# An explicit order for 1944 steps of a two-filter S4 mix, paired sines over two PSUM banks, and no sine product on GpSimd

## The chip, the cores and the metric

The kernel runs on one core of one Trainium2 chip. The metric is the device time of one execution in microseconds (us); the median of several runs is compared. The profile and the trace show one further execution.

## The reference, cut to what matters

Two state-space filters, A (S4) and B (S4D), act on the same signal x of 2048 positions and 512 channels; a sigmoid gate per position mixes the results.

```python
P = jnp.exp(logdA[:, :, None] * l[None, None, :])      # 512 channels x 128 modes x 2048 positions
K = jnp.einsum("dn,dnl,dn->dl", Cc, P, dB).real        # the filter of A; B alike, with 2 * C
Uf = rfft(up); Kf = rfft(Kp)                           # both padded to 2 * L
y = irfft(Uf * Kf)[:, :L] + u * Dskip
g = _sigmoid((x * gate_w).sum(-1, keepdims=True))
return g * a + (1 - g) * b
```

The bulk of the work is to build the filter K, 512 x 2048 sums over 128 complex modes, and the long convolution of x with it. All of it is float32.

## The kernel before, in words

**Tiling.** The 512 channels are cut into four quarters q of 128 channels. Each quarter has two filters k (0 is A, 1 is B), so there are eight units (q, k). A unit's 128 channels are worked in eight chunks of 16 channels. The 128 modes lie on the partitions. A position is split as 64 j + s, so that the exponential at a position is a product of two tables, one over 32 values of j (an angle times j, and a decay) and one over 64 values of s. The sum over the modes then is a matmul of two tables.

**A chunk** (`chunk`, from line 519) runs over all engines. GpSimd writes the two angle tables into a buffer `x` (lines 553 and 562, int32, 512 columns each) and the decay tables into a buffer `E` (lines 573 and 581, 512 and 1024 columns). ScalarE takes four sines of 512 columns: `sf` and `sc` of the angles (lines 591 and 592), then the absolute value in place (line 593, 1024 columns), then `cf` and `cc`, the cosines by a shifted sine (lines 595 and 599). Three of the four go to PSUM buffers `ps`. VectorE multiplies them by the decays: two products of `sf` into `Qt` (lines 603 and 606), one of `sc` into `Dt` (line 612), a double one of `cf` into `Pt` (line 616, 1024 columns) and one of `cc` into `Ct` (line 621). In 28 of the 64 chunks, chosen by the bit masks `DP`, `sc` goes to an SBUF buffer `scs` and GpSimd makes `Dt` from it. TensorE then forms the filter's values (`products`, line 638, 32 small matmuls) and adds the skip term with one matmul by the identity (line 647). ScalarE copies the result to `K` (line 657): 25 pairs of chunks share one copy of 512 columns, 14 chunks have one of 256 for themselves.

**The convolution.** `put` (line 689) transforms K over the 32 rows; its two banks are copied to a buffer `F` (line 704) by ScalarE (52 copies) or VectorE (44), by the masks `EV` and `EU`. `forward` (line 717) transforms over the columns, in eight groups `mg` of a unit; `stage2` loads the signal's transform `U` by DMA (line 772), multiplies on VectorE (lines 773 and 776), transforms back (lines 784 and 785) and copies to `F` on ScalarE (line 790). `final` transposes on VectorE (line 806), makes the last transform (line 812) and applies the gate: ScalarE (line 826), VectorE (lines 828 and 889). The signal itself goes through `stage1_u` and `stage2_u` once for each quarter; its transform is copied by VectorE (line 744, 16) or ScalarE (line 746, 16) and kept in DRAM. The parameters of a quarter, angles and amplitudes of its modes, are worked out by `params_t`, `params_c`, `anchors` and `weights`: some 28 small VectorE instructions for each quarter (lines 351 to 453), and exponentials on ScalarE (line 496), which need another activation table than the sines.

**What sets the order.** All steps are first only recorded by `op`, with engine, assumed cost, a due date, and the buffers read and written. `Plan.run` then plays a list schedule: on each engine the step with the earliest due date whose inputs and buffers are free by the assumed costs goes next. That order is the program; each engine works its steps strictly in it, and the semaphores are put in from the tiles that two steps share. The due dates come from a line per unit (`TO`, `LAG`, `FSP`, `YSP` and others). PSUM is eight tiles `ps` of 128 x 512 float32, a bank each; a step's buffer is picked in `Plan.run`.

Of the kernel before, what the change touches and what calls it, by code (L numbers as in the profile page):

```python
# [18 lines left out]
EV = (120, 86, 87, 147, 87, 144, 180, 65)  # L19
EU = (106, 60, 170, 40)  # L20
# [4 lines left out]
CX = 0.269  # L25
TO = (-0.43, -0.23, -0.25, 0.14, 0.07, 0.08, 0.07, -0.0)
NK = 6
NZ = 4
FE = (0, 6, 14, 0)
KP = (3, 4, 4, 3, 1, 4, 3, 3)  # L30
NST = 4
NGH = 2
ZU = (249, 188, 2, 216)
WV = 0
# [10 lines left out]
    "F": (4096, 3), "AB": (28 * NCH, 2), "x": (1024, 2), "E": (1536, 2), "Qt": (1024, 2), "Dt": (512, 2),  # L45
    "Pt": (1024, 1), "Ct": (512, 1), "scs": (512, 1), "K": (512, 2), "z": (512, 4), "U": (1024, 2),
    "st": (512, 3), "p": (256, 5), "dtb": (256, 2), "pi": (512, 2), "pf": (256, 2), "al": (256, 3), "fi": (256, 2), "gh": (NCK * HC * 12, 1), "ps": (512, 8),
}
SC = 4
KG = 2  # L50
KH = 4

CAPS = {"sc": SC, "kg": KG, "kh": KH, "fb": 8}
LAT = {'T': 0.51, 'A': 0.29, 'V': 0.14, 'G': 1.05, 'D': 0.78}
SWITCH = 0.29
LAG = (1.3, 0.68, 0.64, 0.83, 0.35, -0.05, 0.65, 0.86)
FSP = (0.4, 0.89, 1.11, 0.56, 0.87, 1.93, 0.72, -0.65)
YSP = (1.36, 0.72, 0.01, 1.32, 1.12, 0.7, 2.26, 0.77)
UDS = (0.39, 0.61, 3.7, -1.59)
USP = (-0.94, -1.13, 1.71, -0.48)  # L60
GD = 2.687
GSP = 0.397
DP = (4, 93, 146, 253, 41, 150, 74, 132)
GWD = -7.0
TWD = 5.474
UAHEAD = 0.322
UPRE = 0.932
WPRE = 1.454
AC = 5.612
AC2 = 3.768  # L70
PT = 3.053
PC = 1.603
CA = 0.212
CV = 0.253
CD = -0.256
CK = 0.49
CE = 0.176
CS = 0.293
FW = 0.083
# [22 lines left out]
class Op:  # L102
    __slots__ = ("eng", "cost", "due", "fn", "deps", "bufs", "func", "nbytes", "wait", "end", "succ", "start", "lag", "unit")
# [6 lines left out]
class Plan:  # L110
# [3 lines left out]
    def __init__(self):  # L114
        self.ops = []
        self.unit = None

    def op(self, eng, cost, due, fn, r=(), w=(), func=None, nbytes=0, after=(), hold=()):
        o = Op()
        o.eng, o.cost, o.due, o.fn, o.func, o.nbytes = eng, cost, round(due, 6), fn, func, nbytes  # L120
        o.deps, o.bufs = set(after), []
        for items, wr in ((r, False), (w, True)):
# [11 lines left out]
        o.unit = self.unit  # L134
# [4 lines left out]
        return o  # L139

# [88 lines left out]
def gated_s4_mix(ctx: ExitStack, tc: tile.TileContext, ins: dict, out: bass.AP):  # L229
# [11 lines left out]
        t: [(ps if t == "ps" else sb).tile([P, n], F32, tag=f"{t}{i}", name=f"{t}{i}") for i in range(m)]  # L241
        for t, (n, m) in SLOTS.items()
    }

# [8 lines left out]
    def each(eng, due, fns, r=(), w=()):  # L253
        for cost, fn in fns:
            op(eng, cost, due, fn, r=r, w=w)
# [22 lines left out]
    load_params(0, -9.8)  # L278
# [4 lines left out]
    gw, gwB = load("gate_w", [P, NQ], -0.8)  # L283
    w1i, w1iB = load("c_w1i", [P, 64], -0.7)
    Gw, GwB = load("c_g", [P, NJ, P], GWD)
    Tw, TwB = load("c_t", [P, NJ, 192], TWD)

# [53 lines left out]
    def params_t(q, due):  # L341
# [7 lines left out]
        def diag():  # L349
# [18 lines left out]
            (0.35, lambda: V.scalar_tensor_tensor(_flat(th()), _flat(th()), 1.0 / (2 * PI), b.t[:, 0:256], ALU.mult, ALU.mult)),  # L368
            (0.35, lambda: V.tensor_scalar(h(), th(), MAGIC, MAGIC, ALU.add, ALU.subtract)),
            (0.35, lambda: V.tensor_tensor(h(), th(), h(), ALU.subtract)),  # L370
            (0.35, lambda: V.tensor_scalar(piv()[:, :, :, 0], h(), TWO32 / 2, None, ALU.mult)),

            (0.35, lambda: V.tensor_scalar(t(), h(), MAGIC / 64, None, ALU.add)),
            (0.35, lambda: V.scalar_tensor_tensor(_flat(h()), _flat(t()), MAGIC / 64, _flat(h()), ALU.subtract, ALU.subtract)),
            (0.35, lambda: V.tensor_scalar(piv()[:, :, :, 1], h(), -64 * TWO32, None, ALU.mult)),
# [11 lines left out]
    def params_c(q, due):  # L387
# [16 lines left out]
        op("G", 2.2, due, prod, w=[rows, t0, t1])  # L404
# [3 lines left out]
        def sizes():  # L408
# [6 lines left out]
            (0.35, lambda: V.tensor_tensor(p3(t0), aa(), b0(), ALU.max)),  # L415
            (0.35, lambda: V.tensor_tensor(b1(), aa(), b0(), ALU.min)),
            (0.35, lambda: V.tensor_tensor(p3(t2), b0(), aa(), ALU.is_gt)),
            (0.35, lambda: V.tensor_scalar(b0(), p3(t0), 1e-37, None, ALU.max)),
            (1.67, lambda: V.reciprocal(aa(), b0())),
            (0.35, lambda: V.tensor_tensor(aa(), b1(), aa(), ALU.mult)),  # L420
# [3 lines left out]
        def angle():  # L424
# [11 lines left out]
            (0.35, lambda: V.tensor_tensor(ee(), b1(), ee(), ALU.mult)),  # L436
            (0.35, lambda: V.tensor_tensor(b0(), p3(t0), b0(), ALU.mult)),
            (0.35, lambda: V.tensor_tensor(b1(), b0(), ee(), ALU.add)),
            (0.22, lambda: V.scalar_tensor_tensor(ee()[:, 0, :], b1()[:, 0, :], 1.0, p3(dtb)[:, 0, :], ALU.mult, ALU.mult)),
            (0.22, lambda: V.scalar_tensor_tensor(ee()[:, 1, :], b1()[:, 1, :], 2.0, p3(dtb)[:, 1, :], ALU.mult, ALU.mult)),  # L440
# [4 lines left out]
            (0.35, lambda: V.tensor_scalar(x0(), aa(), -1.0 / PI, 0.25, ALU.mult, ALU.add)),  # L445
            (0.35, lambda: V.tensor_tensor(x0(), x0(), x2(), ALU.mult)),
            (0.35, lambda: V.scalar_tensor_tensor(aa(), aa(), 0.5 / PI, x0(), ALU.mult, ALU.add)),
            (0.35, lambda: V.tensor_scalar(x0(), aa(), -2.0, 0.5, ALU.mult, ALU.add)),
            (0.35, lambda: V.scalar_tensor_tensor(x0(), cr(), 0.0, x0(), ALU.is_lt, ALU.mult)),
            (0.35, lambda: V.tensor_tensor(aa(), aa(), x0(), ALU.add)),  # L450
            (0.35, lambda: V.tensor_scalar(x0(), ci(), 0.0, -2.0, ALU.is_lt, ALU.mult)),
            (0.35, lambda: V.scalar_tensor_tensor(b1(), x0(), 1.0, aa(), ALU.add, ALU.mult)),  # L452
            (0.35, lambda: V.tensor_scalar(fi.v("n (k c) -> n k c", dt=I32, k=2, c=NCH), b1(), TWO32, None, ALU.mult)),
# [13 lines left out]
        op("G", 3.5, due, middle, r=[d["pi"], tmB], w=[t1, fi])  # L467
# [3 lines left out]
    anch, step, Kt, kgs, first = {}, {}, {}, [None], [None]  # L471
# [34 lines left out]
    def weights(q, k, due):  # L506
        b, _, AA, _ = anch[q, k]
        d = prm[q]
        eng = V if WV else G
        op(  # L510
            "V" if WV else "G", 0.61 if WV else 1.0, due,
            lambda: eng.tensor_tensor(
# [5 lines left out]
    def chunk(q, k, c, due):  # L518
# [5 lines left out]
        x, E, Qt, Dt, Pt, Ct = (Buf(t) for t in ("x", "E", "Qt", "Dt", "Pt", "Ct"))  # L524
        on_pool = DP[2 * q + k] >> c & 1
        sf, cf, cc = bank("sc"), bank("sc"), bank("sc")
        sc = Buf("scs") if on_pool else bank("sc")
# [3 lines left out]
        qv = lambda b: b.v("n (c w t) -> n c w t", c=NCK, w=2, t=NJ)  # L531

# [122 lines left out]
        if not last:  # L655
            return
# [426 lines left out]
```

## Time and profile before

| | |
|---|---|
| median of 3 runs | 520.92 us (518.69 to 522.67) |
| profiled execution, its own time | 523.36 us |
| its span, first to last instruction | 521.6 us, so 1.8 us lie around it |
| mean granted TensorE clock | 0.905 |

PE is TensorE's matmul, PEld its weight load, DVE is VectorE, ACT ScalarE, POOL GpSimd, and SP issues the DMAs. A group row gives line, engine, operation, written and read tiles, shapes and count, then the busy time and the mean duration of one in ns, then the idle time of the engine just before and what ended it. The windows view gives the busy time of each engine in a stretch, with the number of instructions in brackets. The waits view says which engine stood still, at which line, for whom, how many us in total, how often, and the longest. A row of the timeline has start, duration, engine, line and tiles.

### The profile page before, as it was taken

What the parts mean: (1) busy time and instruction counts of PE and PEld (TensorE: products, weight loads), DVE (VectorE), ACT (ScalarE), POOL (GpSimd) and SP (SyncE); (2) the same over time, 40 slices, a digit from 0 to 9 for tenths busy, and PEclk for the clock granted to TensorE, in tenths of its full rate; (3) what the DMA queues carried; (4) which work ended last, traced back from release to release, by engine and by line L of the source; (5) the groups of instructions that cost most, each with busy time, mean ns of one, the idle gap of its engine ahead of it and who ended that gap; (6) DMA issues with size and microseconds to landing.
All of it is one profiled execution on the core that took longest, in us unless ns stands there. A gap on an engine that the chain in (4) does not pass through costs nothing.

```text
span 521.6 us, 21373 instructions
## 1 busy us (share of the span) xinstructions
PE 424.9 (81%) x9254; PEld 369.7 (71%) x9254; DVE 443.7 (85%) x737; ACT 418.3 (80%) x786; POOL 419.8 (80%) x365
## 2 busy tenths in 40 slices
PE   2685969749869885399898999597969997999993
PEld 1685859649869752296797698587659776997881
DVE  6657799878998988979769899889999899999844
ACT  4978697759999867989799898878999996786134
POOL 3377999895999999659999899977999899996003
PEclk9876997969969999599999799889978997999998
DMA  8954552624304564334452746042334441443532
GB/s 287 362 177 131 183 181 83 206 78 130 120 2 137 178 213 154 128 124 162 148 193 83 242 137 208 32 120 87 104 103 142 151 138 43 128 155 102 193 119 81
DMA packets 35759, 74.91 MB, mean 144 GB/s; under 512 B 3792, under 2 KB 4176, under 8 KB 35408
## 3 DMA queue, kind: packets, MB, share of 16 engines
q1 hardware_dynamic: 35664, 73.54, 42.6%
q8 instruction: 72, 1.18, 1.0%
q14 instruction: 23, 0.19, 0.1%
HBM read 53.60 MB, written 19.92 MB: 141 GB/s over the span
## 4 chain that ended last, share of the span: by engine, by line
PE 36%; DVE 23%; ACT 22%; DMA 8%; issue 7%; POOL 3%; SPq 1%; POOLq 0%; DVEq 0%; ACTq 0%
PE ps L638 7%; PE ps L689 7%; PE ps L717 6%; PE ps L784 6%; PE ps L785 5%; ACT AB L496 4%; PE ps L812 4%; DVE Pt L616 3%; ACT x L593 3%; DVE F L806 3%; DMA U<-ud 2%; DVE Ct L621 2%; DMA U<-in_u 2%; DVE z L776 2%; DVE Qt L603 2%
## 5 line engine op out<-in xcount | busy, mean ns | idle before, releaser
L581 POOL TENSOR_TENSOR E<-AB 128x1024 f32<-128x1024 f32 x64 | 125.4, 1960 | 1.2 <-DVE Ct L621 1.1
L717 PE MATMUL ps<-F,c_g 128*128 128x128 f32 x768 | 111.3, 299 | 16.3 <-ACT AB L428 4.1
L717 PEld LDWEIGHTS ps<-F,c_g 128*128 128x128 f32 x768 | 102.1, 209 | 21.7 <-ACT F L704 6.2
L784 PE MATMUL ps<-z,c_t 128*128 128x128 f32 x512 | 102.6, 282 | 3.6 <-DVE z L776 1.6
L785 PE MATMUL ps<-z,c_t 128*128 128x128 f32 x512 | 99.2, 275 | 0.3 <-DVE z L776 0.2
L638 PE MATMUL ps<-Pt,Ct 128*32 128x64 f32 x2048 | 70.0, 233 | 23.1 <-DVE Ct L621 20.5
L784 PEld LDWEIGHTS ps<-z,c_t 128*128 128x128 f32 x512 | 77.5, 191 | 11.0 <-DVE z L776 2.9
L616 DVE TENSOR_TENSOR Pt<-ps,E 128x1024 f32<-128x1024 f32 x64 | 77.7, 1213 | 8.4 <-PE ps L638 5.6
L562 POOL TENSOR_TENSOR x<-pi,c_tm 128x512 int32<-128x512 int32 x64 | 67.9, 1062 | 20.9 <-ACT ps L595 18.8
L785 PEld LDWEIGHTS ps<-z,c_t 128*128 128x128 f32 x512 | 77.7, 192 | 0.7 <-DVE z L776 0.7
L638 PEld LDWEIGHTS ps<-Pt,Ct 128*32 128x32 f32 x2048 | 49.7, 117 | 34.1 <-DVE Ct L621 18.6
L573 POOL TENSOR_TENSOR E<-AB 128x512 f32<-128x512 f32 x64 | 68.6, 1073 | 4.3 <-ACT AB L496 2.4
L638 PE MATMUL ps<-Qt,Dt 128*32 128x64 f32 x2048 | 68.7, 231 | 1.0 <-issue 0.9
L593 ACT ACTIVATE x<-x 128x1024 f32<-128x1024 int32 x64 | 67.8, 1059 | 1.8
L553 POOL TENSOR_TENSOR x<-gh 128x512 int32<-128x512 int32 x64 | 68.5, 1071 | 0.5 <-ACT ps L599 0.4
L689 PE MATMUL ps<-w,K 64*64 64x64 f32 x2048 | 46.9, 243 | 21.8 <-DVE Pt L616 10.3
L689 PEld LDWEIGHTS ps<-w,K 64*64 64x64 f32 x2048 | 40.6, 154 | 29.6 <-DVE Pt L616 10.8
L773 DVE TENSOR_TENSOR z<-ps,U 128x512 f32<-128x512 f32 x64 | 43.6, 681 | 17.2 <-DMA U<-ud 11.3
L496 ACT ACTIVATE AB<-al 128x128 f32<-128x128 f32 (+1 forms) x160 | 55.3, 530 | 1.5 <-DVE ps L452 1.4
L790 ACT COPY F<-ps 128x512 f32<-128x512 f32 x64 | 37.0, 585 | 23.5 <-PE ps L785 23.2
L638 PEld LDWEIGHTS ps<-Qt,Dt 128*32 128x32 f32 x2048 | 52.2, 118 | 1.4 <-issue 1.4
L612 POOL TENSOR_TENSOR Dt<-scs,E 128x512 f32<-128x512 f32 x28 | 35.9, 1284 | 16.4 <-issue 8.2
(112 smaller groups left out, 840.0 us busy)
## 6 DMA issues: line engine op xcount, KB each, us to landing
U<-ud SPq DMA_DIRECT2D x64, 512.0 KB, 3.7
ud<-z SPq DMA_DIRECT2D x32, 256.0 KB, 3.2
U<-in_u SPq DMA_DIRECT2D x16, 256.0 KB, 5.0
ud<-z SPq DMA_DIRECT2D x32, 128.0 KB, 3.2
U<-in_uT SPq DMA_DIRECT2D x8, 512.0 KB, 3.9
c_t<-in_c_t SPq DMA_DIRECT2D x1, 3072.0 KB, 16.2
w<-st SPq DMA_DIRECT2D x12, 256.0 KB, 2.3
st<-w SPq DMA_DIRECT2D x12, 256.0 KB, 2.7
```

What stands on the lines that cost most here:

```text
L496: A.activation(dst()[..., i], src(), AF.Exp, scale=sg * float(t0 + dt * i))
L553: G.tensor_tensor(xi()[:, :, 1, :].rearrange("n c (a b) -> n c a b", a=4), t[:, :, 0:4].unsqueeze(3).to_broadcast([P, NCK, 4, 8]), t[:, :, ...
L562: lambda: G.tensor_tensor(xi()[:, :, 0, :], d["piv"]()[:, k, ch, 0].unsqueeze(2).to_broadcast([P, NCK, NJ]), tm[:, 0:NJ].unsqueeze(1).to_b ...
L573: G.tensor_tensor(Ev()[:, :, 0, :].rearrange("n c (a b) -> n c a b", a=4), A1()[:, ch, ::-1].unsqueeze(3).to_broadcast([P, NCK, 4, 8]), BB ...
L581: G.tensor_tensor(Ev()[:, :, 1:3, :].rearrange("n c w t -> n c (w t)"), AA()[:, ch].rearrange("n c w a -> n (c w) a").unsqueeze(3).to_broa ...
L593: op("A", 1.02, e, lambda: A.activation(x.t, x.v(dt=I32), AF.Abs), w=[x])
L616: lambda: V.tensor_tensor(qv(Pt), tv(cf).unsqueeze(2).to_broadcast([P, NCK, 2, NJ]), Ev()[:, :, 0:2, :], ALU.mult),
L638: T.matmul(K4[32 * b : 32 * b + 32, g, :], tv(lw)[:, 4 * g + b, :], qv(rw)[:, 4 * g + b].rearrange("n h t -> n (h t)"), start=(lw is Ct an ...
L689: T.matmul(hs[h].t[64 * d : 64 * d + 64, 256 * i + 64 * g : 256 * i + 64 * g + 64], Kv[r, g, :], w1[r, d, 64 * h : 64 * h + 64], start=Tru ...
L717: T.matmul(pairs(b.t[:, NCH * mm : NCH * mm + NCH]), Gw[:, 4 * mg + mm, :], Fv(F)[:, :, 4 * mg + mm, :], start=True, stop=True,)
L784: T.matmul(hb.t[:, cs], Tw[:, m, 0:128], Z1.t[:, cs], start=True, stop=False)
L785: T.matmul(hb.t[:, cs], Tw[:, m, 64:192], Z2.t[:, cs], start=False, stop=True)
```

## The change

1. `PLACES`, a list of 1944 numbers, gives each recorded step its place in one overall order (`placed`); the number of recorded steps is 1944 too, so that the list schedule is not run. Dues for each group replace the lines per unit, but with the list they set nothing.
2. `sf` and `sc` are made by one sine of 1024 columns, and `cf` and `cc` by another. To write two banks with one instruction, PSUM is now one tile `banks` of 8 x 512 columns, and the output is a strided view of banks i and j.
3. `outer` makes the first half of the old `Qt` and `Dt` in one VectorE instruction over the two banks; the buffers become one, `QD`. No chunk has its `Dt` on GpSimd, and `scs` is gone.
4. All chunks go in pairs: 32 copies to `K` of 512 columns. The skip term takes four matmuls of 32 columns for each pair in place of one by the whole identity.
5. The masks are redrawn: of the copies to `F` VectorE makes 29 and ScalarE 67; of those of the signal's transform 12 and 20; VectorE gates 4 tiles where it gated 7, and ScalarE 3 more.

The program has 681 VectorE instructions (739 before), 680 on ScalarE (788), 342 on GpSimd (370), and 28 loads of an activation table (32). Its core:

```diff
-    "F": (4096, 3), ..., "E": (1536, 2), "Qt": (1024, 2), "Dt": (512, 2),
-    "Pt": (1024, 1), "Ct": (512, 1), "scs": (512, 1), "K": (512, 2), ...
+    "F": (4096, 3), ..., "E": (1536, 2), "QD": (1536, 2),
+    "Pt": (1024, 1), "Ct": (512, 1), "K": (512, 2), ...
+PLACES = (
+    0, 2, 3, 50, 5, 77, 256, 142, 40, 126, 19, 1, 76, 6, 7, 8, 15, 16, 22, 23, 26, 27, 28, 43, 44, 11, 17, 34, 62, 18,
...
+    def placed(self):
+        order = [o for _, o in sorted(zip(PLACES, self.ops), key=lambda p: p[0])]
...
+            for b in o.bufs:
+                if b.tag and b.slot is None:
+                    l = free[b.tag]
+                    till = {i: max([lag(e, t) for e, t in ends.items()] + [0.0]) for i, ends in l.items()}
+                    b.slot = min(sorted(till), key=till.get)
...
+    banks = ps.tile([P, 8, 512], F32, tag="ps", name="ps")
+    pl.tiles["ps"] = [banks[:, i, :] for i in range(8)]
...
+        def two_banks(a, b):
+            i, j = min(a.slot, b.slot), max(a.slot, b.slot)
+            return banks[:, i : j + 1 : j - i, :].rearrange("n w (c t) -> n w c t", c=NCK), 1 if a.slot < b.slot else -1
...
-        op("A", 0.56, e, lambda: A.activation(tv(sf), xi()[:, :, 0, :], AF.Sin, scale=SCL), r=[(x, h0)], w=[sf], func="S")
-        op("A", 0.53, e, lambda: A.activation(tv(sc), xi()[:, :, 1, :], AF.Sin, scale=SCL), r=[(x, h1)], w=[sc], func="S")
+        def sines(a, b, **kw):
+            o, d = two_banks(a, b)
+            A.activation(o, (xi() if a is sf else qv(x))[:, :, ::d, :].rearrange("n c w t -> n w c t"), AF.Sin, **kw)
+        op("A", 1.0, e, lambda: sines(sf, sc, scale=SCL), r=[x], w=[sf, sc], func="S", chain="sf")
         op("A", 1.02, e, lambda: A.activation(x.t, x.v(dt=I32), AF.Abs), w=[x])
+        op("A", 1.0, e, lambda: sines(cf, cc, bias=HALF_PI, scale=-SCL), r=[x], w=[cf, cc], func="S", chain="cf")
...
-        op("V", 0.61, e, lambda: V.tensor_tensor(qv(Qt)[:, :, 0, :], tv(sf), Ev()[:, :, 0, :], ALU.mult), r=[sf, (E, h0)], w=[(Qt, h0)])
+        def outer():
+            i, d = two_banks(sf, sc)
+            w = slice(0, 3, 2) if d > 0 else slice(2, None, -2)
+            V.tensor_tensor(
+                QDv()[:, :, w, :].rearrange("n c w t -> n w c t"), i, Ev()[:, :, w, :].rearrange("n c w t -> n w c t"), ALU.mult
+            )
+        op("V", 1.13, e, outer, r=[sf, sc, (E, h0), (E, ((2, 3),))], w=[(QD, h0), (QD, ((2, 3),))], chain="Q0")
...
-        eng = G if on_pool else V
-            "G" if on_pool else "V", 1.23 if on_pool else 0.61, due + CD if on_pool else e,
-            lambda: eng.tensor_tensor(tv(Dt), tv(sc), Ev()[:, :, 2, :], ALU.mult), r=[sc, (E, ((2, 3),))], w=[Dt],
...
+            if i:
+                for b in range(4):
+                    T.matmul(
+                        kg.v("n (c s) -> n c s", c=8, s=NS)[32 * b : 32 * b + 32, :, 31],
+                        ident[:, 32 * b : 32 * b + 32],
+                        tap[:, 2 * q + k, 4 * (c - 1) : 4 * (c + 1)],
...
-    order = pl.run()
+    order = pl.placed() if len(PLACES) == len(pl.ops) else pl.run()
```

**How it moves instructions, at three places.** The first is on ScalarE, in the middle of the program, with the engines that each row waits for in brackets (L591 to L599 are the sines, L593 and L786 the absolute value, L704, L790, L900 and L984 copies to `F`). Before:

```order
L591 ACTIVATE ps_115<-x_71 128x512 [waits DVE_49,Pool_49]
L592 ACTIVATE scs_81<-x_71 128x512 [waits Pool_49]
L593 ACTIVATE x_71<-x_71 128x1024 [waits Activation_49]
L704 COPY F_67<-ps_114 128x8x64 [waits PE_49]
L790 COPY F_66<-ps_112 128x64x8
L704 COPY F_67<-ps_116 128x8x64 [waits DVE_49,PE_49]
L595 ACTIVATE ps_112<-x_71 128x512 [waits Activation_49]
L657 COPY K_83<-ps_110 128x512 [waits PE_49]
L599 ACTIVATE ps_115<-x_71 128x512 [waits DVE_49]
```

and now, L783 being a pair of sines:

```order
L783 ACTIVATE ps<-x_71 128x2x512 [waits PE_49,DVE_49,Activation_49,Pool_49]
L900 COPY F_66<-ps 128x8x64 [waits Activation_49]
L786 ACTIVATE x_71<-x_71 128x1024 [waits Activation_49]
L783 ACTIVATE ps<-x_71 128x2x512 [waits DVE_49,PE_49,Activation_49]
L900 COPY F_66<-ps 128x8x64 [waits PE_49,Activation_49]
L847 COPY K_79<-ps 128x512 [waits PE_49]
L783 ACTIVATE ps<-x_72 128x2x512 [waits DVE_49,Pool_49]
```

Five rows of a chunk have become three, and the sines now wait for TensorE as well: 64 of the 128 pairs do (ten of them at a table load just ahead), where 5 of the 256 single sines did. The view of banks i and j is guarded as one range: of the waits between two PSUM accesses in the new program 319 are between instructions that share no bank, one of them lying between the other's i and j.

The second place is VectorE at the end of the second quarter's first unit, where the parameters of the third quarter begin (L368 to L380 before, L553 to L565 now). Before:

```order
L616 TENSOR_TENSOR Pt_79<-ps_117,E_74 128x1024
L621 TENSOR_TENSOR Ct_80<-ps_117,E_74 128x512
L380 TENSOR_TENSOR al_105<-AB_70,ps_112 128x128
L368 SCALAR_TENSOR_TENSOR AB_70<-AB_70,ps_112 128x256
L369 TENSOR_SCALAR ps_112<-AB_70 128x256
L370 TENSOR_TENSOR ps_112<-AB_70,ps_112 128x256
L371 TENSOR_SCALAR pi_100<-ps_112 128x256
L373 TENSOR_SCALAR p_94<-ps_112 128x256
L374 SCALAR_TENSOR_TENSOR ps_112<-p_94,ps_112 128x256
L375 TENSOR_SCALAR pi_100<-ps_112 128x256
L806 STREAM_TRANSPOSE F_67<-F_67 128x8x2x32
```

and now:

```order
L565 TENSOR_TENSOR al_101<-AB_70,ps 128x128
L553 SCALAR_TENSOR_TENSOR AB_70<-AB_70,ps 128x256
L554 TENSOR_SCALAR ps<-AB_70 128x256
L555 TENSOR_TENSOR ps<-AB_70,ps 128x256
L810 TENSOR_TENSOR Ct_78<-ps,E_74 128x512
L556 TENSOR_SCALAR pi_97<-ps 128x256
L558 TENSOR_SCALAR p_90<-ps 128x256
L805 TENSOR_TENSOR Pt_77<-ps,E_74 128x1024
L559 SCALAR_TENSOR_TENSOR ps<-p_90,ps 128x256
L793 TENSOR_TENSOR QD_75<-ps,E_73 128x2x16x32
L560 TENSOR_SCALAR pi_97<-ps 128x256
```

The run of eight dependent parameter steps is broken up by the products of the next chunks (L793, L805, L810).

The third place is TensorE at the last chunk of all, where the rest of the last unit begins (L638 and L822 are the products, L647 and L832 the skip term, L689 and L883 the `put` transform, L812 and L1006 the last transform of the unit before, L717 and L912 `forward`). Before:

```order
L638 MATMUL ps_110<-Qt_76,Dt_77 32x64 x4
L647 MATMUL ps_110<-dskip,c_id 128x4
L812 MATMUL ps_113<-F_67,c_w1i 64x512 x2
L689 MATMUL ps_115<-w_129,K_82 64x64
L689 MATMUL ps_112<-w_129,K_82 64x64
```

(the two L689 rows alternate for 16 matmuls in all, and L717 follows) and now:

```order
L822 MATMUL ps<-QD_76 32x64 x4
L832 MATMUL ps<-dskip,c_id 32x8 x4
L883 MATMUL ps<-w_119,K_80 64x64 x16
L883 MATMUL ps<-w_119,K_79 64x64 x32
L912 MATMUL ps<-F_67,c_g 128x128 x8
L1006 MATMUL ps<-F_68,c_w1i 64x512 x2
L912 MATMUL ps<-F_67,c_g 128x128 x4
```

Behind the last products stand 48 `put` matmuls where there were 16, and three of the four L1006 steps of the unit before where there was one L812 step.

More of the change, by code (lines that the diff above doesn't have):

```diff
@@ L82, in _flat, with _on_dve @@
+EV = (78, 44, 0, 64, 0, 48, 0, 160)
+ZU = (107, 170, 4, 96)
+FE = (0, 4, 0, 8)
+PLACES = (
[93 rows of a table added]
+)
+def _on_dve(masks, i, bit):
+    return masks[i] >> bit & 1
 def _flat(t):
@@ L102 @@
 class Op:
-    __slots__ = ("eng", "cost", "due", "fn", "deps", "bufs", "func", "nbytes", "wait", "end", "succ", "start", "lag", "unit")
+    __slots__ = ("eng", "cost", "due", "fn", "deps", "bufs", "func", "nbytes", "wait", "end", "succ", "start", "lag")
 def _meet(a, b):
@@ L114, in __init__, with op @@
     def __init__(self):
-        self.ops = []
-        self.unit = None
-    def op(self, eng, cost, due, fn, r=(), w=(), func=None, nbytes=0, after=(), hold=()):
+        self.ops, self.last = [], {}
+    def op(self, eng, cost, due, fn, r=(), w=(), func=None, nbytes=0, after=(), hold=(), chain=None):
         o = Op()
@@ L121, in op @@
         o.deps, o.bufs = set(after), []
+        if chain:
+            o.deps |= {self.last[chain]} if chain in self.last else set()
+            self.last[chain] = o
         for items, wr in ((r, False), (w, True)):
@@ L465, in middle @@
             G.tensor_tensor(f, f, x, ALU.add)
-        op("G", 3.5, due, middle, r=[d["pi"], tmB], w=[t1, fi])
+        op("G", 1.6, due, middle, r=[d["pi"], tmB], w=[t1, fi])
         d["fi"] = fi
-    anch, step, Kt, kgs, first = {}, {}, {}, [None], [None]
+    anch, step, Kt, kgs = {}, {}, {}, [None]
     def anchors(q, k, due):
@@ L523, in chunk @@
         h0, h1, h12 = ((0, 1),), ((1, 2),), ((1, 3),)
[L524 to L527, printed above, removed]
+        x, E, QD, Pt, Ct = (Buf(t) for t in ("x", "E", "QD", "Pt", "Ct"))
+        sf, sc, cf, cc = (bank("sc") for _ in range(4))
         xi = lambda: x.v("n (c w j) -> n c w j", dt=I32, c=NCK, w=2, j=NJ)
@@ L673, in gated_s4_mix, with put @@
     halves = {}
-    def put(F, K, items, c, due, on_dve):
+    def put(F, K, items, c, due, masks):
         if c % 2 == 0:
```

414 lines of the change are left out of this document (214 added, 200 removed), and 120 rows, old and new, of tables (CH, PLACES, S2, TN).

## The prediction

> **What bounds the kernel now.** I read the page first, then busy time by stretch, then the chain, then the waits.
>
> ```profile
> span 521.6 us, 21373 instructions
> PE 424.9 (81%) x9254; PEld 369.7 (71%) x9254; DVE 443.7 (85%) x737; ACT 418.3 (80%) x786; POOL 419.8 (80%) x365
> PE 36%; DVE 23%; ACT 22%; DMA 8%; issue 7%; POOL 3%; SPq 1%; POOLq 0%; DVEq 0%; ACTq 0%
> ```
>
> The first two rows are the span and the busy times, the third the chain that ended last, by engine. Four engines lie within 26 us of each other, and none stands alone on the chain. The fullest, DVE, sets a floor of 443.7; the other 77.9 us of the span are its idle time. Where they lie, the windows view tells:
>
> ```profile
> core 0: us, PE busy (x) PEld busy (x) DVE busy (x) ACT busy (x) POOL busy (x), PEclk, DMA share, GB/s
> 0.00:40.00 40.00, 24.54 (x458) 22.11 (x458) 25.07 (x63) 28.66 (x71) 19.66 (x29) 0.87 0.77 275
> 40.00:480.00 440.00, 367.85 (x8485) 321.06 (x8488) 393.25 (x631) 376.22 (x674) 396.22 (x333) 0.90 0.41 133
> 360.00:480.00 120.00, 107.74 (x2499) 93.31 (x2502) 116.18 (x186) 104.76 (x177) 113.93 (x93) 0.93 0.36 117
> 480.00:521.60 41.60, 32.49 (x326) 26.49 (x315) 25.35 (x45) 13.41 (x42) 3.93 (x3) 0.95 0.39 134
> ```
>
> DVE stands idle for 14.9 us in the head (parameters, first loads), 46.7 in the long middle and 16.3 in the tail. In the middle DVE and POOL are both busy for 90%. In its last 120 us DVE is idle for only 3.8 (3.2%); in the 320 before that, for 42.9 (13%). The waits view of the whole run:
>
> ```profile
> DVE F L704 <- PE ps L689: 13.0, 15, 3.1
> DVE z L773 <- DMA U<-ud: 11.3, 12, 1.9
> DVE Pt L616 <- PE ps L638: 5.6, 6, 2.8
> ACT F L790 <- PE ps L785: 23.2, 18, 5.9
> ACT F L704 <- PE ps L689: 6.5, 8, 1.4
> POOL x L562 <- ACT ps L595: 18.8, 6, 6.1
> SPq L772 <- DVE z L776: 187.9, 48, 19.4
> ```
>
> No wait of DVE is large by itself; they are the slack of an order that doesn't quite fit. So the change can gain in two ways: less work on DVE, or less of the 46.7.
>
> **The change part by part: work.** Steps come from start to start in the timeline, since neighbours overlap.
>
> ```profile
> 444.24 0.68 DVE L612 TENSOR_TENSOR Dt<-ps,E 128x512 f32<-128x512 f32 x1
> 444.84 1.21 DVE L616 TENSOR_TENSOR Pt<-ps,E 128x1024 f32<-128x1024 f32 x1
> 445.97 0.68 DVE L621 TENSOR_TENSOR Ct<-ps,E 128x512 f32<-128x512 f32 x1
> 453.34 0.68 DVE L704 COPY F<-ps 128x512 f32<-128x512 f32 x1
> 453.94 0.74 DVE L776 SCALAR_TENSOR_TENSOR z<-ps,sgn,U 128x512 f32<-128x512 f32 x1
> 447.68 1.29 POOL L612 TENSOR_TENSOR Dt<-scs,E 128x512 f32<-128x512 f32 x1
> 448.93 1.06 POOL L562 TENSOR_TENSOR x<-pi,c_tm 128x512 int32<-128x512 int32 x1
> L612 POOL TENSOR_TENSOR Dt<-scs,E 128x512 f32<-128x512 f32 x28 | 35.9, 1284 | 16.4 <-issue 8.2 <-ACT scs L592 4.4 <-POOL x L562 1.7
> ```
>
> A DVE product of 512 columns takes a step of 0.60 (444.24 to 444.84), one of 1024 takes 1.13. The fused product isn't in this trace; L616 reads one bank, twice over. I bound it by 1.06 (twice the 0.53 that the second 512 columns add) and 1.21 (L616's whole duration), and take 1.13, L616's step. In the 28 chunks that had Dt on POOL DVE then pays 1.13 for 0.60, +14.8; in the other 36 it pays 1.13 for 1.20, -2.5. The masks take 15 + 4 copies and 3 gatings of 0.60 from it: -13.2. **DVE: -0.9** (-5.4 to +4.2 by the bounds). POOL loses 28 steps of 1.25: **-35.0**.
>
> ```profile
> 452.81 1.06 ACT L593 ACTIVATE x<-x 128x1024 f32<-128x1024 int32 x1
> 453.77 0.57 ACT L704 COPY F<-ps 128x512 f32<-128x512 f32 x1
> 454.38 0.60 ACT L595 ACTIVATE ps<-x 128x512 f32<-128x512 f32 x1
> 454.91 0.58 ACT L599 ACTIVATE ps<-x 128x512 f32<-128x512 f32 x1
> 457.95 0.59 ACT L790 COPY F<-ps 128x512 f32<-128x512 f32 x1
> 458.43 0.61 ACT L592 ACTIVATE ps<-x 128x512 f32<-128x512 int32 x1
> 507.97 3.21 ACT L826 ACTIVATE F<-ps,gs 128x128 f32<-128x128 f32 x12 [0.43 <-PE ps L812]
> L496 ACT ACT_TABLE_LOAD x11 | 14.1, 1283 | 0.2
> ```
>
> On ACT a sine's step is 0.53. The paired sine isn't there either: L593, as wide, steps 0.96 (452.81 to 453.77); its ends are that and 1.06, two single steps. I take 0.96: 128 x (0.96 - 1.06) = -12.8, or 0. Table loads, 4 fewer: -5.1. Taken over: 15 + 4 copies of 0.48, 12 gatings of 0.27: +12.3; copies to K are even. **ACT: -5.6**. All this is off the sum while ACT has its 103 us of idle time; with that cover gone it would be worth at most its own 5.6.
>
> The Trainium skill (ScalarE: Activation LUTs, "What ACT_TABLE_LOAD costs") adds a drain of some 1.38 us to each switch of tables; by that ACT would save 10.6 and not 5.1. The row above shows loads of 1283 ns with 0.2 us idle before all eleven, so the trace doesn't show the drain, and either way the saving lies in ACT's idle time.
>
> The four skip matmuls are narrower than the one before; I put PE at 0, and 425 of 522 hides an error of some us. SP issues the same 205 DMAs in a new order. U's loads stood behind DVE's L776 for 187.9 us, since there are two buffers for U, and there still are; so the 11.3 us that DVE lost to U count as middle, below.
>
> **Part by part: order.** Head: the parameter chain is the same; 0. Tail: it begins when the last chunk's products are done. There the order puts two more `rows` steps and two more `put` steps than before:
>
> ```profile
> 480.92 1.08 PE L812 MATMUL ps<-F,c_w1i 128*64 128x512 f32 x4
> 481.93 0.69 PE L689 MATMUL ps<-w,K 64*64 64x64 f32 x32
> ```
>
> PE paces the tail (32.5 of 41.6 busy, DVE 25.4), so 2 x 1.01 (480.92 to 481.93) and 2 x 0.55 or so come on top: **+3.1**, or nothing if PE was going to wait for U's DMA there.
>
> Middle: the 46.7 idle us of DVE could stay (0), or shrink to the 3.2% of the last 120 us, which leaves 14.0 (-32.7). Three things speak for a good part of it. DVE's copies to F, which stood 13.0 us for PE, fall from 44 to 29. POOL, the other engine at 90%, falls to 82% ((396.2 - 35.0) / 440), so it can work ahead of ACT and DVE; it also no longer stands at a Dt (16.4 us idle in its row) with the next chunk's x and E queued behind it. And the parameter runs, which held up the products, are broken up. I take three quarters: **-24**.
>
> Against it stand new waits. A paired sine is guarded over the whole range of banks between its two, and 64 of the 128 wait for PE, where 5 single ones did. Queued behind a waiting sine are ACT's copies to F and K, and PE and DVE wait for those. The nearest rows are ACT's other waits for PE: L704's 50 waiting rows lost 6.5 us, 0.13 each, and L790's 54 lost 23.2, 0.43 each. That gives 8.3 to 27.5 us on ACT, and below that nothing, if PE is always ahead. I take **+8.3**: ACT has idle time for the rest.
>
> The Trainium skill (PSUM — Partial Sum Buffer, "PSUM bank collisions raise a hardware error") asks for a guard by bank and quadrant. By that a pair would owe a wait to the users of its own two banks alone, this term would be 0, and the span 499.8; the waits in the built program go further, and no run so far prices them.
>
> **Sum** on the profiled execution: 521.6 - 0.9 + 3.1 - 24 + 8.3 = 508.1 us of span, 0.974 of it. On the median, 520.92 (the profiled execution itself took 523.36, 0.5% above it), that is **507.5 us**.
>
> **Rivals.**
>
> *The bank ranges decide (slower).* The 64 waits cost 0.43 each and ACT's copies pass it on: 521.6 - 0.9 + 3.1 - 24 + 27.5 = 527.3, 526.6 on the median. It decides from about 0.37 us a wait on, where the gain of 24 is gone. For it: the waits are in the program, and 44 more of PE's waits for ACT and 50 of DVE's share no bank with what they wait for. Against it: most of L704's kind were short. If DVE's 50 cost 0.2 each too, it is 536.
>
> *DVE binds as before (no change).* Its work is even, -0.9, and the new order merely moves its idle time: 521.6 - 0.9 + 3.1 = 523.8, 523.1 on the median; with a few us of gain still within 1%. For it: 393 of 440 with every engine near it, so that each stall passes on. Against it: the last 120 us show that 97% can be had.
>
> *The order fits (much faster).* All of the middle goes at 3.2% idle and the new waits find PE ahead: 521.6 - 0.9 + 3.1 - 32.7 = 491.1, 490.4 on the median. For it: the last 120 us did it with POOL at 95%, and POOL is relieved. Against it: those 120 us hold no parameter chain.
>
> That the change doesn't do what it says is ruled out: the list has as many places as there are steps, and the built order is the new one.
>
> **How the numbers follow.** The forecast (500 to 515) has 0.37, the better fit 0.21, no change 0.19, the bank ranges 0.23. A measurement of this kernel can tell about 1% from no change. So faster by over 1% (below 515.7) has 0.58, within 1% 0.19, slower 0.23. The range takes in the better fit down to 487 and the bank ranges up to 532; the forecast's own is 500 to 515.
>
> **What would show it.** Work: L783 at 1.04 to 1.06 us of duration, the fused product at 1.2, DVE busy for 443, ACT for 413, POOL for 385, 28 table loads. Order: DVE idle between 40 us and the last product for some 25 to 35 us where it was 46.7. Waits: in the view of waits, L783 for PE at some 8 us in all; 25 or more would show the first rival. The last L822 products at about 464 us (480.6 before) would be the gain; the stretch behind them at 42 to 45 us the tail. It would be wrong if the fused product took over 1.25 us (DVE then gains 7.7), if DVE's idle time in the middle stayed at 45, or if the sines' waits came to more than the copies to F lost before.

## The result and the profile after

| | before | after |
|---|---|---|
| median | 521.09 us (518.69 to 522.67, 4 runs) | 698.10 us (696.99 to 699.53, 4 runs) |
| ratio to before, 95% interval | | 1.3404 [1.3345, 1.3463] |
| span of the profiled execution | 521.6 us | 697.5 us |
| mean granted TensorE clock in it | 0.905 | 0.842 |

The forecast was 507.5 us, in a range of 487 to 532. The kernel became a third slower. The page of after, its span, its busy times, and the chain that ended last:

```profile
span 697.5 us, 21438 instructions
PE 475.0 (68%) x9432; PEld 405.1 (58%) x9432; DVE 447.7 (64%) x679; ACT 412.0 (59%) x678; POOL 386.3 (55%) x337
...
PE 14%; DVE 9%; ACT 6%; issue 2%; POOL 1%; DMA 1%; POOLq 0%; ACTq 0%; DVEq 0%
```

The chain's shares add up to only a third of the span, so it isn't used below. The work of DVE, ACT and POOL is that of the forecast (443, 413, 385) within 5 us. DVE's idle time is 249.8 us (697.5 less 447.7) where it was 77.9, so nearly all of what was lost was lost in waiting. No engine is above 68%. The windows view, cut at 40 us and at the last products:

```profile
core 0: us, PE busy (x) PEld busy (x) DVE busy (x) ACT busy (x) POOL busy (x), PEclk, DMA share, GB/s
0.00:40.00 40.00, 21.59 (x666) 19.34 (x666) 26.80 (x63) 27.36 (x63) 18.99 (x29) 0.87 0.63 233
40.00:651.00 611.00, 416.59 (x8438) 357.59 (x8442) 392.35 (x563) 371.16 (x576) 363.33 (x306) 0.84 0.30 98
651.00:697.50 46.50, 36.84 (x344) 28.18 (x332) 28.51 (x54) 13.49 (x41) 4.01 (x3) 0.91 0.39 125
```

Head and tail are nearly what they were (the tail is some 5 us longer). The loss lies in the middle, where DVE, ACT and POOL are each busy for only some 60 to 64%, and PE for 68%. The waits view, with total us, number of times and the longest:

```profile
POOL x L751 <- ACT ps L783: 158.3, 38, 15.0
...
ACT F L984 <- PE ps L979: 45.6, 14, 10.6
DVE QD L793 <- ACT ps L783: 31.3, 15, 4.6
DVE Pt L805 <- ACT ps L783: 24.0, 19, 4.5
ACT ps L783 <- DVE QD L793: 23.1, 13, 4.7
PEld ps L978 <- ACT ps L783: 21.8, 9, 4.1
ACT ps L783 <- PE ps L912: 19.3, 7, 4.7
...
PE ps L978 <- ACT ps L783: 16.7, 8, 4.0
...
ACT ps L783 <- PE ps L883: 14.7, 7, 4.9
```

Line 783 (the paired sine) and line 793 (the fused product), the two instructions that use a view of two banks, stand on one side of most of the large waits. They wait for each other, for PE's `forward` (L912) and `put` (L883), and PE's second transform (L978) waits for them. L978, L912 and L883 have no data in common with a sine. The groups, with the idle time ahead of each:

```profile
L783 ACT ACTIVATE ps<-x 128x1024 f32<-128x1024 int32 (+1 forms) x128 | 131.5, 1029 | 132.5 <-DVE QD L793 23.1 <-PE ps L912 19.3 <-DVE z L970 15.0
L912 PE MATMUL ps<-F,c_g 128*128 128x128 f32 x768 | 127.8, 323 | 45.9 <-ACT ps L783 14.7 <-DVE QD L793 9.5 <-DVE F L900 4.9
...
L793 DVE TENSOR_TENSOR QD<-ps,E 128x1024 f32<-128x1024 f32 x64 | 78.1, 1220 | 67.1 <-ACT ps L783 31.3 <-PE ps L979 16.2 <-PE ps L912 7.6
```

One of these waits in the timeline, with ACT, DVE, PE and POOL side by side:

```profile
91.88 2.02 PE L912 MATMUL ps<-F,c_g 128*128 128x128 f32 x8
...
93.98 1.03 ACT L783 ACTIVATE ps<-x 128x1024 f32<-128x1024 f32 x1 [3.87 <-PE ps L912]
...
95.04 1.23 DVE L805 TENSOR_TENSOR Pt<-ps,E 128x1024 f32<-128x1024 f32 x1 [4.46 <-ACT ps L783]
95.06 1.65 PE L912 MATMUL ps<-F,c_g 128*128 128x128 f32 x6 [1.17 <-ACT ps L783]
95.09 1.06 POOL L751 TENSOR_TENSOR x<-pi,c_tm 128x512 int32<-128x512 int32 x1 [2.05 <-ACT ps L783]
```

In the built program this sine writes banks 0 and 6, and L912 at 91.88 writes bank 3. ACT stands 3.87 us until PE is done with a bank that the sine doesn't touch. Then PE's next L912, which writes bank 2, stands 1.17 us until the sine is done. DVE and POOL wait for the sine with good reason, but for a sine that came late. Below, a wait between two instructions that use PSUM and have no bank in common is called a *foreign* wait. The built program has 319 of them (none before): 175 held by ScalarE's instructions, 75 by VectorE's, 69 by TensorE's.

### The profile page after: what moved, and what is told of

It is laid out like the page before. It is cut to its first block, busy times and chain, and to the rows that moved or that the text cites. A ratio compares the mean times of both kernels' runs of the same rounds, so it can differ in the third digit from the quotient of the medians.

```text
span 697.5 us, 21438 instructions
## 1 busy us (share of the span) xinstructions
PE 475.0 (68%) x9432; PEld 405.1 (58%) x9432; DVE 447.7 (64%) x679; ACT 412.0 (59%) x678; POOL 386.3 (55%) x337
## 5 line engine op out<-in xcount | busy, mean ns | idle before, releaser
L783 ACT ACTIVATE ps<-x 128x1024 f32<-128x1024 int32 (+1 forms) x128 | 131.5, 1029 | 132.5 <-DVE QD L793 23.1
L912 PE MATMUL ps<-F,c_g 128*128 128x128 f32 x768 | 127.8, 323 | 45.9 <-ACT ps L783 14.7
L978 PE MATMUL ps<-z,c_t 128*128 128x128 f32 x512 | 119.0, 319 | 48.0 <-ACT ps L783 16.7
L912 PEld LDWEIGHTS ps<-F,c_g 128*128 128x128 f32 x768 | 114.6, 230 | 63.4 <-ACT ps L783 16.4
L978 PEld LDWEIGHTS ps<-z,c_t 128*128 128x128 f32 x512 | 91.5, 223 | 60.6 <-ACT ps L783 21.8
L793 DVE TENSOR_TENSOR QD<-ps,E 128x1024 f32<-128x1024 f32 x64 | 78.1, 1220 | 67.1 <-ACT ps L783 31.3
L979 PE MATMUL ps<-z,c_t 128*128 128x128 f32 x512 | 113.0, 307 | 1.0 <-DVE z L970 0.8
L822 PE MATMUL ps<-Pt,Ct 128*32 128x64 f32 x2048 | 72.9, 241 | 40.5 <-DVE QD L793 12.7
L805 DVE TENSOR_TENSOR Pt<-ps,E 128x1024 f32<-128x1024 f32 x64 | 78.0, 1218 | 26.4 <-ACT ps L783 24.0
L979 PEld LDWEIGHTS ps<-z,c_t 128*128 128x128 f32 x512 | 91.3, 223 | 1.9 <-DVE z L970 1.9
L822 PEld LDWEIGHTS ps<-Pt,Ct 128*32 128x32 f32 x2048 | 51.2, 121 | 52.8 <-DVE QD L793 13.7
L984 ACT COPY F<-ps 128x512 f32<-128x512 f32 x64 | 36.4, 588 | 63.3 <-PE ps L979 45.6
L822 PE MATMUL ps<-QD 128*32 128x64 f32 x2048 | 71.8, 238 | 2.9 <-issue 2.9
L883 PE MATMUL ps<-w,K 64*64 64x64 f32 x2048 | 49.3, 246 | 34.5 <-ACT ps L783 12.9
L970 DVE SCALAR_TENSOR_TENSOR z<-ps,sgn,U 128x512 f32<-128x512 f32 x64 | 47.4, 743 | 37.3 <-ACT ps L783 15.3
L786 ACT ACTIVATE x<-x 128x1024 f32<-128x1024 int32 x64 | 67.8, 1060 | 1.3
L883 PEld LDWEIGHTS ps<-w,K 64*64 64x64 f32 x2048 | 41.8, 155 | 45.3 <-ACT ps L783 13.9
```

The source lines that it names most:

```text
L783: A.activation(o, (xi() if a is sf else qv(x))[:, :, ::d, :].rearrange("n c w t -> n w c t"), AF.Sin, **kw)
L786: op("A", 1.02, e, lambda: A.activation(x.t, x.v(dt=I32), AF.Abs), w=[x])
L793: V.tensor_tensor(QDv()[:, :, w, :].rearrange("n c w t -> n w c t"), i, Ev()[:, :, w, :].rearrange("n c w t -> n w c t"), ALU.mult)
L805: lambda: V.tensor_tensor(qv(Pt), tv(cf).unsqueeze(2).to_broadcast([P, NCK, 2, NJ]), Ev()[:, :, 0:2, :], ALU.mult),
L822: T.matmul(K4[32 * b : 32 * b + 32, g, :], lw[:, 4 * g + b, :], rw[:, 4 * g + b].rearrange("n h t -> n (h t)"), start=(z + g + i == 0), st ...
L883: T.matmul(hs[h].t[64 * d : 64 * d + 64, 256 * i + 64 * g : 256 * i + 64 * g + 64], Kv[r, g, :], w1[r, d, 64 * h : 64 * h + 64], start=Tru ...
```

## The experiments

**Theory.** The view `banks[:, i : j + 1 : j - i, :]` is guarded from bank i to bank j. Pairs lie up to seven banks apart (only 28 of the 128 sine pairs are on neighbours), and the foreign waits that follow make the whole loss. **Rivals:** the written order itself leaves engines waiting; two banks filled by one instruction cost something wherever they lie; one PSUM tile costs something in itself.

**1. One-bank instructions, eight tiles.** The order and each buffer's bank stay; foreign waits: none.

```diff
-    banks = ps.tile([P, 8, 512], F32, tag="ps", name="ps")
-    pl.tiles["ps"] = [banks[:, i, :] for i in range(8)]
+    pl.tiles["ps"] = [ps.tile([P, 512], F32, tag=f"ps{i}", name=f"ps{i}") for i in range(8)]
...
-            o, d = two_banks(a, b)
-            A.activation(o, (xi() if a is sf else qv(x))[:, :, ::d, :].rearrange("n c w t -> n w c t"), AF.Sin, **kw)
+            for w, o in enumerate((a, b)):
+                A.activation(tv(o), (xi() if a is sf else qv(x))[:, :, w, :], AF.Sin, **kw)
...
+            for w, o in ((0, sf), (2, sc)):
+                V.tensor_tensor(QDv()[:, :, w, :], tv(o), Ev()[:, :, w, :], ALU.mult)
```

> The order of the 1944 steps and the bank of every buffer are those of the change; only each paired sine and each fused sine product is written as two instructions of one bank each (128 more on ScalarE, 64 more on VectorE), and the eight banks are eight tiles again. Ranges theory (a view of banks i and j is guarded over all banks between them, and instructions wait for work on banks that they do not touch; that is the whole loss): the 319 waits between instructions that share no bank are gone, VectorE's idle time falls from 249.8 us to under 70, and the time to 495-520 us. Order theory (the written order itself leaves the engines waiting): 660-700 us, VectorE idle still over 210. Pairing theory (what costs is that two banks are filled and freed together, not which banks): 600-690 us, since the two halves still stand one right behind the other.

Measured: **504.92 us** (503.73 to 507.94), 0.9691 [0.9633, 0.9748] of before. Its page:

```profile
span 503.7 us, 21750 instructions
...
PE 411.9 (82%) x9432; PEld 351.7 (70%) x9432; DVE 444.7 (88%) x743; ACT 418.4 (83%) x806; POOL 385.4 (77%) x337
```

The same order with the same banks, and DVE's idle time is 59.0 us. The order theory falls, and the theory of pairs is left only where one instruction fills both.

**2. The same in one tile.** As above, but without the first three lines of that diff.

> As the run with eight tiles, but the eight banks stay one tile of 8 x 512, each instruction touching one bank of it. Ranges theory: a view of one bank is guarded as one bank, so the same 495-520 us and within 1% of the run with eight tiles. Rival (a single tile is itself guarded or freed as a whole, whatever the view): 650-700 us.

Measured in a single execution: 515.0 us. That lies in the first range, but 2% over the run with eight tiles, where at most 1% was expected. With repeated executions:

> The kernel of the run with one tile and split instructions again, now timed: it stood at 515.0 us in one look, 2% over the same order in eight tiles (504.9 us). If one tile in itself costs nothing (the pairs on neighbours, in one tile, took 505.3 us): 503-508 us, and the one look was off. If the 63 further waits that one tile brings between instructions of one bank cost what it showed: 512-518 us.

Measured: 507.12 us (504.00 to 509.80), 0.9731 [0.9674, 0.9788]. The medians of one tile and of eight lie 2.2 us apart and the intervals overlap, so a cost of the single tile isn't shown. A single execution can thus be some 8 us off (515.0 against 507.12).

**3. Pairs on neighbouring banks.** All instructions of the change, its order too; only bank numbers come from a table.

```diff
+BANKS = (
...
-                    b.slot = min(sorted(till), key=till.get)
+                    b.slot = next(banks) if b.tag == "ps" else min(sorted(till), key=till.get)
```

> The order and every instruction are those of the change; only the bank numbers differ: they come from a table that gives 127 of the 128 sine pairs two neighbouring banks (one pair has one bank between), where the change had 28 of 128 on neighbours. Ranges theory: with no bank between, nothing is guarded that is not touched: 490-510 us, some 5 us under the run with split instructions, L783 waiting for TensorE under 15 us. Order theory and pairing theory: both halves of every pair are as before, 660-700 us.

Measured: **505.26 us** (502.54 to 510.64), 0.9673 [0.9624, 0.9723]. The page and three groups:

```profile
span 503.2 us, 21449 instructions
...
PE 413.4 (82%) x9432; PEld 353.5 (70%) x9432; DVE 441.7 (88%) x679; ACT 407.2 (81%) x678; POOL 385.0 (77%) x337
```

```profile
L805 ACT ACTIVATE ps<-x 128x1024 f32<-128x1024 int32 (+1 forms) x128 | 132.1, 1033 | 26.3 <-DVE Pt L827 5.0 <-DVE z L965 4.4 <-DVE QD L815 3.6
L934 PE MATMUL ps<-F,c_g 128*128 128x128 f32 x768 | 107.5, 288 | 17.7 <-ACT F L922 6.1 <-DVE fi L660 3.7 <-DVE F L922 2.3
...
L815 DVE TENSOR_TENSOR QD<-ps,E 128x1024 f32<-128x1024 f32 x64 | 77.9, 1217 | 0.8 <-ACT ps L805 0.4 <-issue 0.2 <-POOL E L792 0.2
```

L805 is the paired sine here: its idle time went from 132.5 to 26.3 us, and TensorE no longer stands among its three largest releasers. The fused product (L815) fell from 67.1 to 0.8. A table of bank numbers gave back 192.8 us. This is the shown cause.

**4. The due dates with the pairs.** `placed` is replaced by `run`.

```diff
-    order = pl.placed() if len(PLACES) == len(pl.ops) else pl.run()
+    order = pl.run()
```

> The instructions are those of the change, pairs over two banks included, but the list of places is not used: the steps are ordered by the due dates that the file still holds, with the caps of 4, 2, 3 and 8 banks. The pairs lie as far apart as in the change (325 waits between instructions that share no bank, against 319). Ranges theory: 640-710 us, like the change. Order theory: the list of places was at fault, so 520-560 us.

Measured in one execution: 704.64 us, as the ranges theory said. With the cure of the first run:

> The run by due dates (704.6 us) with the cure of the first run: eight tiles, every sine and fused product as two instructions of one bank; 325 foreign waits become none. It tells what the list of places itself is worth, set against the run with the list and the same cure (504.9 us). At 0.61 us per wait this order comes to 704.6 - 0.61 x 325 = 506 us, so the list would be worth nothing. If the list carries the gain over the kernel before, 520 us or more. If the due dates that the file still holds were left unfitted when the list came, 540 us or more, and the single waits of that order would then have cost less than 0.61 us each.

Measured in one execution: 576.36 us, the third of the three expectations. The list is worth 71 us against the due dates that the file still holds; nothing follows for due dates that were fitted, as before's were. The 325 foreign waits of this order cost 128.3 us, 0.39 each, less than the 0.61 of the change.

**5. How the loss grows with the number of foreign waits.** Four kernels in the order of the change: only the sines in two instructions; only the products; and pairs two and four banks apart by a table.

> Order and banks of the change, the eight banks in one tile; each paired sine is written as two instructions of one bank, the fused sine product on VectorE still reads two banks in one view. Of the 319 waits between instructions without a common bank 110 are left, all with a fused product on one side. If every such wait costs the same (698.1 less 505.3 us over 319 less 2 waits = 0.61 us), 505 + 0.61 x 108 = 571 us. If the sines alone make the loss (they stall ScalarE, which feeds the rest), 505-520 us. If the fused product is as bad by itself, 600 us or more.

> The other half: paired sines over two banks as in the change, the fused sine product written as two instructions of one bank each. 262 of the 319 waits are left, all with a sine on one side. At 0.61 us for each, 505 + 0.61 x 260 = 664 us. If the sines alone make the loss, 690-700 us. If the fused product makes most of it, under 600 us.

> Order and instructions of the change; the table of banks puts 127 of the 128 pairs two apart, with one bank between, and one pair three apart. 196 waits between instructions without a common bank (the change: 319, neighbours: 2). Ranges theory at 0.61 us for each: 505 + 0.61 x 194 = 623 us. If only far pairs hurt (a wait on one foreign bank is mostly over by then), 505-550 us.

> As the run before, with 119 of the 128 pairs four apart, five three apart and four five apart: three banks between, 449 waits between instructions without a common bank. Ranges theory at 0.61 us for each: 505 + 0.61 x 447 = 778 us. If the loss saturates, because the engines already work in turns, 700-730 us.

| kernel | foreign waits | expected at 0.61 each | measured, us | DVE idle, us | us per foreign wait over the neighbours |
|---|---|---|---|---|---|
| pairs on neighbours | 2 | | 505.26 | 61.5 | |
| only sines split | 110 | 571 | 575.73 | 129.0 | 0.65 |
| one bank between | 196 | 623 | 607.60 | 159.9 | 0.53 |
| only products split | 262 | 664 | 643.65 | 191.0 | 0.53 |
| the change | 319 | | 698.10 | 249.8 | 0.61 |
| three banks between | 449 | 778 | 787.99 | 334.9 | 0.63 |

The four new kernels ran once each. An error of 8 us would move their prices by 0.02 to 0.07 us.

Neither the sines nor the products make the loss alone, and it doesn't saturate. Whichever instruction stands on one side, a foreign wait costs 0.53 to 0.65 us of the kernel's time in this order.

**6. Pairs in the order before.** Where two sines of a pair follow each other on ScalarE, they are one instruction over the banks they already had (53 pairs), in one tile.

```diff
...
+        p, q = sorted((o0, o1), key=at.get)
+        if behind[p] is q and not any(p in o.deps for o in order[at[p] : at[q]]):
+            p.fn, q.fn = (lambda: None), fn
```

> The kernel before with its own order and its own banks; the eight banks are one tile, and where the two sines of a pair stand one behind the other on ScalarE with nothing between that reads the first, they are one instruction over two banks (53 pairs, 1 to 7 banks apart). That makes 93 waits between instructions without a common bank, in an order that was not part of the change. Ranges theory at 0.61 us per wait, less some 2 us for 53 instructions fewer: 521 + 57 - 2 = 576 us. If the loss takes the order of the change as well, 518-530 us.

Measured in one execution: 562.80 us, 41.9 above before and 13 below the 576 expected: 0.45 for each of 93. The pairs' row:

```profile
L598 ACT ACTIVATE ps<-x 128x1024 f32<-128x1024 f32 (+1 forms) x53 | 54.5, 1028 | 59.2 <-PE ps L797 10.6 <-PE ps L659 9.9 <-PE ps L729 7.2
```

The mechanism needs nothing of the new order: here 53 pairs stand for 59.2 us, and the three largest waits are for PE.

**7. What the relief of GpSimd is worth.** First in the kernel before, VectorE making the 28 products of `scs`:

```diff
-        eng = G if on_pool else V
+        eng = V
```

> The kernel before, in its order; the 28 products of the sine that GpSimd makes are made by VectorE at the same place of the order. GpSimd has 28 x 1.23 = 34 us less to do, VectorE 28 x 0.6 = 17 us more. If VectorE bounds the kernel before with little slack, 530-540 us. If VectorE's idle time is due to a late GpSimd, as the prediction has it for 24 us of the middle, 510-518 us.

Measured: 540.66 us (535.59 to 543.20), 1.0365 [1.03, 1.043]. This run doesn't separate the two, since VectorE's work didn't grow by 17 us but by 25.1. Its idle time fell from 77.9 to 65.0 us, which the heavier VectorE or the lighter GpSimd may have done. The line's answer (min, median and max of the duration in ns):

```profile
L612 DVE TENSOR_TENSOR Dt<-ps,E x36: 666/681/693, 40.0 to 484.2; 128x512 f32<-128x512 f32 x36
...
L612 DVE TENSOR_TENSOR Dt<-scs,E x28: 662/975/1968, 48.2 to 487.1; 128x512 f32<-128x512 f32 x28
```

With both operands in SBUF the same product takes up to 1968 ns; the last section shows why. So the question was put the other way round, in the first run's kernel: the 28 products back on GpSimd.

```diff
...
+            V.tensor_tensor(QDv()[:, :, 0, :], tv(sf), Ev()[:, :, 0, :], ALU.mult)
+            eng, o = (G, side) if on_pool else (V, tv(sc))
+            eng.tensor_tensor(QDv()[:, :, 2, :], o, Ev()[:, :, 2, :], ALU.mult)
```

> The first run's kernel (order and banks of the change, one-bank instructions, eight tiles, 504.9 us) with one edit of the change undone: the 28 chunks that had their sc product on GpSimd before have it there again, from a sine in the one SBUF buffer, at the same place of the order. GpSimd gets 28 x 1.25 = 35 us more (420 us), VectorE 28 x 0.60 = 17 us less. If the relief of GpSimd makes the gain, as the prediction's middle term has it: 515-525 us, VectorE's idle time up by 25-35 us. If VectorE's work bounds the new order: 490-497 us. If GpSimd, which now waits for a sine with the next tables queued behind, runs late: over 525 us.

Measured: 518.67 us (515.46 to 523.53), 0.9958 [0.9919, 0.9996] of before. Its page:

```profile
span 513.3 us, 21698 instructions
...
PE 413.4 (81%) x9432; PEld 355.9 (69%) x9432; DVE 430.6 (84%) x715; ACT 419.0 (82%) x806; POOL 419.4 (82%) x365
```

VectorE has 14.1 us less to do than in the first run and stands idle for 82.7 us in place of 59.0. The kernel takes 13.8 us longer. Most of the new idle time is for the decay tables `E`, which GpSimd now makes later: L773, the `above` table, is waited for 17 us by the products, and in the first run there is no such wait. The waits view:

```profile
DVE QD L804 <- POOL E L773: 9.2, 9, 2.2
...
DVE Pt L809 <- POOL E L773: 3.2, 2, 2.3
DVE QD L799 <- POOL E L773: 3.0, 4, 1.2
```

In this order, then, a relieved GpSimd is worth more than a relieved VectorE. The order was written without these products. In the kernel before, whose order has them, VectorE's waits for `E` came to 0.5 us, so one that is written with them can be expected to lose less than 13.8 us; no run shows how much less.

## Why the prediction was wrong

**The failed step** is "That gives 8.3 to 27.5 us on ACT ... I take +8.3: ACT has idle time for the rest." The mechanism was named, and as the first rival it had a chance of 0.23 at 527 us. Its size was 192.8 us (698.10 less 505.26), and not 8.3 or 27.5. The waits of the sines for PE alone came to 62.1 us. Their largest, in what the profile tells of line 783 (us, times):

```profile
its engine sat idle before it (us, times) until:
...
  PE ps L912: 19.3, 7
...
  PE ps L883: 14.7, 7
  PE ps L979: 14.6, 4
```

L822 and L832 add 7.2 and 6.3; with pairs on neighbours the largest wait of a sine for PE is 0.9 us. By the prediction, 25 us or more here would show the first rival. Three things went wrong in sizing the term.

1. *The count.* 64 sines that wait for PE were priced, with 50 of DVE's waits as an afterthought. The program has 319 foreign waits, a number that stood on record ahead of the prediction. All were to be counted, since the table above gives much the same price for those with a sine on one side and those with a product. At the rival's own 0.43 us, 319 waits come to 137 us: the count was most of the error.
2. *The price.* It came from the copies L704 and L790, which lost 0.13 and 0.43 us a row waiting for a result that they need, and the order puts a copy where its result should be ready. A foreign wait goes to a step that the order may put *beside* the sine, since the two have nothing in common; it lasts until that step is over, and L912's in the timeline above ran 2.02 us. That this is the reason is argued, from one such wait. The row of the paired sine gives the size: 132.5 us of idle time, for whatever reason, over 128 rows is 1.04 each, against 0.21 with neighbours (26.3 over 128).
3. *The cover.* ACT's 103 us of idle time were to hide the rest. But ACT, DVE and PE all hold foreign waits (175, 75 and 69), in a ring, and a late step makes the next engine's step late, as in the timeline above. DVE's idle time grew by 188.3 us between the neighbours and the change (61.5 to 249.8), and the span by 194.3.

The sentence on the Trainium skill (PSUM — Partial Sum Buffer, "PSUM bank collisions raise a hardware error") gave 499.8 us of span for a guard by bank. With pairs on neighbours the span was 503.2. The runs agree with the rule: the kernels of the first and the third experiment do without guards on the banks between (none and 2 foreign waits), and only the way this program is built adds them.

**The other terms**, read in the kernel with neighbours, where the foreign waits are gone:

- *Work, right.* DVE 441.7 (forecast 442.8), POOL 385.0 (384.8), the fused product 1217 ns (1.2 us); ACT 407.2, 5.5 less than forecast. But 11 us less on ACT bought nothing that these runs can tell: with unpaired sines (418.4) the kernel takes 504.92 in eight tiles and 507.12 in one. That ACT's savings lie in its idle time was right.
- *Middle, right in sum by luck.* The last product starts at 457.4 us (forecast: 464); between 40 and 457.6 DVE is idle for 31.5 us, in the forecast's 25 to 35, and 15.2 below before's 46.7. The forecast was -24 + 8.3 = -15.7. But with the foreign waits gone the 8.3 should be gone too, so the gain of 24 came out as 15.2, under half of the 32.7 and not three quarters. Of its three reasons one was tested, the relief of GpSimd: 13.8 us in the last run, in an order that favours it. For the first, the copies to F stood 9.3 us for PE, where it was 13.0. What the list of places gave by itself wasn't separated.
- *Tail, nearly right.* 45.8 us behind the last product start, 41.2 before: +4.6 for +3.1.
- *Rivals.* "DVE binds as before" (523) and "The order fits" (490) both fail, in the cured kernel too, which lies between them at 505.

The windows view of the kernel with neighbours, cut at the last products:

```profile
0.00:40.00 40.00, 23.32 (x667) 21.39 (x668) 27.15 (x63) 27.41 (x62) 19.92 (x30) 0.79 0.64 233
40.00:457.60 417.60, 354.54 (x8419) 304.53 (x8418) 386.09 (x563) 366.22 (x575) 360.99 (x305) 0.96 0.46 143
457.60:503.20 45.60, 35.58 (x354) 27.62 (x348) 28.47 (x54) 13.62 (x41) 4.08 (x3) 0.98 0.42 128
```

So the range of 487 to 532 held the kernel that the change meant to be, and not the one that it was.

## What to carry to other kernels

When a change writes a strided view over a tile that many steps share, count the waits of the built program between instructions that have nothing in common; a few hundred such waits are no detail, and here each cost 0.4 to 0.65 us of the kernel's time. Price such a wait by the steps that happen to run beside it, not by waits for results that were planned to be ready, and don't let an engine's idle time cover it where the engines wait for each other in a ring. If two buffers are to be filled by one instruction, choose them so that nothing lies between; here a table of bank numbers was worth 193 us, and the same work in instructions of one bank as much.

## What the runs showed of the hardware

- **TensorE's granted clock fell as its work was broken up.** With the same 9432 matmuls in the same order it was 0.947 with 2 foreign waits (PE busy for 82% of the span), 0.915 with 110, 0.881 with 196, 0.868 with 262, 0.842 with 319 (68%) and 0.775 with 449 (66%). The due-date order without a foreign wait had 0.881 at 75%, so it isn't the foreign waits as such. The mean L912 (L934 with neighbours) went from 288 ns to 323 in the change, and PE's busy time from 413.4 to 475.0 us. So part of the price of a foreign wait may be a slower TensorE; no run separates it. The Trainium skill (TensorE: Matmul & The Clock Gate, "What's actually happening") has the clock follow how busy TensorE has lately been; the trace agrees in direction.
- **A VectorE product of two SBUF operands** lasted 662 to 1968 ns (mean 1069) where GpSimd worked beside it, the same product with one operand in PSUM 666 to 693. The Trainium skill (SBUF — State Buffer, "SBUF: two separate sides") has such an instruction lock a port pair that it shares with GpSimd, the other waiting until it is free. The trace agrees. Of the 28 products, 21 began while a GpSimd instruction ran, and each of them ended 0.54 to 0.56 us after that instruction's end; the 7 that began with none running took 0.68 to 0.69 us. The longest, from that run's timeline:

```profile
260.63 1.96 POOL L581 TENSOR_TENSOR E<-AB 128x1024 f32<-128x1024 f32 x1
261.16 1.97 DVE L612 TENSOR_TENSOR Dt<-scs,E 128x512 f32<-128x512 f32 x1
```
